# Batch 1's keys loaded earlier and tile 0's softmax on VectorE, in a chain of attention and two feed-forward layers

## The chip, the cores and the metric

The kernel runs on one core of one Trainium2 chip. The time is the device time of one execution in microseconds (us); lower is better. The core's engines work side by side, each through its own queue in order: TensorE (PE; its weight loads are shown as PEld), VectorE (DVE), ScalarE (ACT), GpSimd (POOL) and SyncE (SP), which issues nearly all transfers.

## The reference

```python
batch, n_heads, seq, head_dim, n_pack = 8, 8, 576, 64, 32
n_tokens, d_model, d_ff = 4608, 512, 2048

def sm_attn(qq, kk, vv):
    s = scale * np.matmul(qq, kk.transpose(0, 1, 3, 2))
    s = s - np.max(s, axis=-1, keepdims=True)
    a = np.exp(s)
    a = a / (np.sum(a, axis=-1, keepdims=True) + 1e-09)
    return np.matmul(a, vv)

p_packed = sm_attn(p, k, v)            # 32 learned queries a head
x = sm_attn(q, p_packed, p_packed)     # 576 queries a head
x = x.transpose(0, 2, 1, 3).reshape(4608, 512)
h = x @ moe_w_in                       # 512 -> 2048
x = (h * np.cos(h)) @ moe_w_out        # 2048 -> 512
h = x @ moe2_w_in
out = (h * np.tanh(softplus(h))) @ moe2_w_out
```

Inputs of attention are float32, the four weight matrices arrive as float64.

## The kernel before

**Tiles and steps.** The tokens of attention and of the first feed-forward layer go in 16 tiles of 288 tokens, two to a batch element. Each tile takes 16 steps, one for each 128 rows of d_ff, so a step is numbered n = 16 t + s. At step n PE computes layer 1 of (t, s) into one of four PSUM banks (`l1`, six matmuls L148 to L150 in `mm3`), ScalarE and VectorE work out h * cos(h) (`chain_first`, `chain_cos`: rounding L913, reduction L915 and L916, sine L922, product L928, which is the last reader of the bank), and three steps later PE does layer 2 (`l2`; for tile 0 in L953). The second feed-forward layer follows all tiles and is not touched.

**Weights by packed keys.** The value matrix of the second attention is folded into w_in: for each batch element, `w_unit` multiplies the packed values PK (L380) with w_in (L577) and splits the product into two halves (L593, L594); `l1` reads these. The float64 weights are turned into float32 by three operations: a Prelu on ScalarE (L520, L620), a shift on VectorE (L522, L621), a merge on VectorE (L526, L625). w_in comes in 16 pieces of 512 KB (L507) through four buffers, w_out in 16 pieces of 512 KB (L608) through the two buffers of `raw`. For tile 0 the merged w_out is used as it is (WM); L630 and L631 split it afterwards for the later tiles.

**Background work.** `k_unit(b, g)` packs the keys and values of four heads: four loads of keys into a `kr` buffer (L153), four loads of p into `pc` (L234), transposes on VectorE (L264, L159), scores on PE (L289), softmax, product with the values. `q_unit(t)` makes a tile's attention weights: scores (L431), transposes (L445), maximum and subtraction (L451, L452), exponential (L459), sum (L463), reciprocal (L466), product (L467), transpose (L471), and a split into a high half on ScalarE (L476) and a low half (L477). `at_ld`, `at_pe` and `at_ew` place each piece at a step; steps below 0 are the prologue. Batch 1's two groups have their stages from steps 13 and 18 on (`K1_OFF`).

**Order.** Within an engine the order is fixed when the program is built, by a planner that works from priorities (`tc.high_priority`) and its own estimate of the times. `tc.issue_after(x)` makes an instruction come later than x in it. `after_w` puts a load behind the last load of weights named so far, for steps up to 20. `behind(key)` does the same with an instruction kept in `marks`; ("act", 1, 0, 1) is the copy of the packed values of batch 0's second group.

Of the kernel before, what the change touches and what calls it, by code (L numbers as in the profile page):

```python
# [8 lines left out]
F32 = mybir.dt.float32  # L9
F32R = mybir.dt.float32r  # L10
I32 = mybir.dt.int32
AF = mybir.ActivationFunctionType
ALU = mybir.AluOpType
# [17 lines left out]
Q_LD = 2  # L31
W_LD = 2
K1_OFF = (13, 18)
K1_LD = 4
W01 = (28, 0.8)
WO_OFF = 0
WO_SPLIT = 13
# [14 lines left out]
Q_SUB0 = (0, 1, 2, 4, 5, 5, 6, 7)  # L52
K_LD0 = 2
Q_LD0 = 2
Q_DVE = (0, 0, 0)
X2_AT = 231
COMB = 240
HOLD_N = 32
# [24 lines left out]
SCALE = 1.0 / math.sqrt(D)  # L83
# [6 lines left out]
def build(tc, q, k, v, p, w1i, w1o, w2i, w2o, out):  # L90
    nc = tc.nc
    ctx = ExitStack()
    with ctx:
# [31 lines left out]
        quarter = wpool.tile([128, 1], F32, name="quarter")  # L125
        nc.vector.memset(quarter, 0.25)
        wpool.tile([128, 8], F32, name="gap_w")
        if WARM:
            warm = wpool.tile([128, 1], F32, name="warm")
# [79 lines left out]
        marks = {}  # L209

        def behind(key):
            ins = marks.get(key)
            return ExitStack() if ins is None else tc.issue_after(getattr(ins, "ins", ins))
# [181 lines left out]
        def q_unit(t, pre=None):  # L395
            st = {}
            b, half = t // 2, t % 2

            def loads():
                if pre:  # L400
                    st["raw"] = early_load(pre([128, 4, 512]), q[b], TT * half * D, False)
                    return
                r = kr_tile([128, 4, 544])
                st["raw"] = [r[:, 0:2], r[:, 2:4]]
                for e in range(2):
                    for g in range(2):
                        o = 64 * g + 32 * e
                        load_half(r[o : o + 32], q[b, 4 * g : 4 * g + 4], TT * half, e)

            def trans(i):  # L410
                if i == 0:
                    st["kt"] = kt_tile([128, 1152])
                trans2(st["kt"][:, 576 * i : 576 * i + 576], st["raw"][i])

            def s0():
                trans(0)

            def s1():
                trans(1)

            def e0_pe():
                st["kt"] = kt_tile([128, 1152])
                for h in range(4):
                    early_copy(st["kt"], early_trans(st["raw"], h, (0, 0, 1)), h, (0, 0, 1))

            def s2_pe():
                st["s"] = [ring() for _ in range(2)]

                def head(g, l):
                    h = PERM[b % 2][l]  # L430
                    return nc.tensor.matmul(  # L431
                        st["s"][g][32 * l : 32 * l + 32, :TT],
                        PK[(b, g)][64 * g : 64 * g + 64, 32 * l : 32 * l + 32],
                        st["kt"][64 * g : 64 * g + 64, TT * h : TT * h + TT],
                        start=True,
                        stop=True,
                    )

                todo = [lambda g=g, l=l: head(g, l) for g, l in sorted(((g, l) for g in range(2) for l in range(4)), key=lambda y: (-PERM[b % 2][y[1]], -y[0]))]
                rounds(st["s"][:1], st["kt"][:, 1152 - HOLD_N :], todo[0], todo[1:])  # L440

            def s2_ew():
                sq = tmp_tile([128, 2, TT])
                for g in range(2):
                    nc.vector.transpose(sq[:, g], st["s"][g][:, :TT])  # L445
                st["sq"] = sq
                st["sv"] = sq.rearrange("p g (a j) -> p (g a) j", j=32)

            def s3():
                mx = ap.tile([128, 18], F32, tag="mx", bufs=2, name=nm("mx"))  # L450
                nc.vector.tensor_reduce(mx, st["sv"], AX.X, ALU.max)  # L451
                (nc.vector if t < Q_DVE[0] else nc.gpsimd).tensor_tensor(st["sv"], st["sv"], mx.unsqueeze(2).to_broadcast([128, 18, 32]), ALU.subtract)  # L452

            def s4():
                with ExitStack() as es:
                    es.enter_context(tc.high_priority(offset=HP_EXP))
                    if CHAIN_EXP and lastexp[0] is not None:
                        es.enter_context(tc.issue_after(getattr(lastexp[0], "ins", lastexp[0])))
                    nc.scalar.activation(st["sq"], st["sq"], AF.Exp, scale=SCALE)  # L459

            def s5():
                sm = ap.tile([128, 18], F32, tag="sq", bufs=2, name=nm("sqs"))
                nc.vector.tensor_reduce(sm, st["sv"], AX.X, ALU.add)  # L463
                nc.vector.tensor_scalar(sm, sm, EPS, None, ALU.add)
                rs = ap.tile([128, 18], F32, tag="rq", bufs=2, name=nm("rq"))
                nc.vector.reciprocal(rs, sm)  # L466
                (nc.vector if t < Q_DVE[1] else nc.gpsimd).tensor_tensor(st["sv"], st["sv"], rs.unsqueeze(2).to_broadcast([128, 18, 32]), ALU.mult)  # L467

            def s6():
                at = tmp_tile([128, 2, TT])  # L470
                nc.vector.transpose(at.rearrange("p g s -> p (g s)"), st["sq"].rearrange("p g s -> p (g s)"))  # L471
                st["at"] = at

            def s7():
                hl = ap.tile([128, 2, 2, TT], F32R, tag="aT", bufs=2, name=nm("aT"))
                nc.scalar.copy(hl[:, 0], st["at"])  # L476
                (nc.vector if t < Q_DVE[2] else nc.gpsimd).tensor_tensor(hl[:, 1], st["at"], hl[:, 0], ALU.subtract)  # L477
                AT[t] = hl

            return loads, [  # L480
                (e0_pe, None) if pre else (None, s0),
                (None, None) if pre else (None, s1),
                (s2_pe, s2_ew),
                (None, s3),
                (None, s4),
                (None, s5),
                (None, s6),
                (None, s7),
            ]

# [109 lines left out]
        WM = []  # L600
        wm_last = [None]

        def wo1_unit(ft):
            st = {}

            def load():
                r = st["r"] = tp.tile([128, 512, 2], I32, tag="raw", bufs=2, name=nm("raw"))
                ins = nc.sync.dma_start(r.rearrange("p f t -> p (f t)"), w1o[128 * ft : 128 * ft + 128, :].bitcast(I32))  # L608
                last_w[0] = getattr(ins, "ins", ins)

            def words():
                if not WM:
                    for i in range(6):
                        x = wo_tile([128, 2, 512], F32)
                        WM.extend((x[:, 0], x[:, 1]))
                if ft == 12:
                    x = wab_tile(1, [128, 4, 512], F32)
                    WM.extend(x[:, i] for i in range(4))
                t = st["t"] = tp.tile([128, 512], I32, tag="tmp", bufs=TMP_BUFS, name=nm("cvt"))
                wm_last[0] = nc.scalar.activation(WM[ft], st["r"][:, :, 1].bitcast(F32), AF.Prelu, scale=2.0**-112, alpha=2.0**32)  # L620
                nc.vector.tensor_scalar(t, st["r"][:, :, 0], 29, None, ALU.logical_shift_right)  # L621

            def merge():
                mi = WM[ft].bitcast(I32)
                nc.vector.scalar_tensor_tensor(mi, mi, 3, st["t"], ALU.logical_shift_left, ALU.bitwise_or)  # L625

            def split():
                w = WO[(1, ft)] = wo_tile([128, 2, 512], F32R)
                with tc.issue_after(getattr(wm_last[0], "ins", wm_last[0])):
                    nc.scalar.copy(w[:, 0], WM[ft])  # L630
                nc.gpsimd.tensor_tensor(w[:, 1], WM[ft], w[:, 0], ALU.subtract)  # L631

            return load, [words, merge], split

        WST = {}
# [126 lines left out]
        def after_w(f, lim=CH_LIM):  # L762
            def run():
                if last_w[0] is None or STEP[0] > lim:
                    return f()
                with tc.issue_after(last_w[0]):
                    f()

            return run
# [7 lines left out]
        def at_ld(n, f):  # L777
            bg_ld.setdefault(n, []).append(f)
# [27 lines left out]
        for g in range(2):  # L806
            wo = lambda sh: wo_tile(sh, F32)
            wa = lambda sh: wab_tile(0, sh, F32)
            loads, vl, stages = k_unit(0, g, wo)
# [4 lines left out]
        loads, stages = q_unit(0, wa)  # L814
# [19 lines left out]
            at_ew(n + WO_SPLIT, split)  # L834
        for g, off in enumerate(K1_OFF):
            loads, vl, stages = k_unit(1, g, ld_tile)
            at_ld(off - K1_LD, after_w(loads))
            for i in range(3):
                at_ld(off + V_LD + i, after_w(vl[i]))
            place(stages, [off + i for i in K1_SUB])  # L840
# [9 lines left out]
        for j, n in enumerate(U_AT):  # L850
            loads, steps = w2o_unit(j)
# [12 lines left out]
        for pair in range(3):  # L864
# [3 lines left out]
            for b, g, off in zip((b0, b0, b0 + 1, b0 + 1), (0, 1, 0, 1), offs):  # L868
                loads, vl, stages = k_unit(b, g, ld_tile)
# [12 lines left out]
        for t in range(1, NT):  # L882
            n = Q_N[t - 1]
            loads, stages = q_unit(t)
# [438 lines left out]
```

## Time and profile before

| | |
|---|---|
| median of 3 runs | 1549.7 us (1548.65 to 1550.8) |
| profiled execution | 1550.71 us, its span in the trace 1548.9 us |
| mean granted TensorE clock | 0.987 |
| PE busy | 1479.0 us, 95% |
| VectorE, ScalarE, GpSimd busy | 71%, 57%, 40% |

An engine's busy time is the sum of its instructions; idle time is given with what ended it ("<-"). The granted clock is the share of full speed that TensorE was allowed.

### The profile page before, as it was taken

The page shows a single profiled execution, that of the slowest core. Times are in us where ns is not written, and L with a number is a line of the kernel's source. Part 1 is how long each engine was busy: PE and PEld are TensorE (multiplying, and loading weights), DVE is VectorE, ACT ScalarE, POOL GpSimd, SP SyncE. Part 2 cuts the span into 40 slices and gives each one's busy share as a digit, 9 for nine tenths or more (in the row PEclk, how much of TensorE's full clock was granted, in tenths as well). Part 3 has the DMA queues.
Part 4 walks back from the last instruction along what each step waited for, and adds up shares of the span by engine and source line. Part 5 has one row for each costly group of instructions (what it writes and reads, how often), then busy time and mean ns, then how long its engine had stood idle before and what let it go on. Part 6 is the DMA issues. An engine that isn't in the chain of part 4 may idle for free.

```text
span 1548.9 us, 28952 instructions
## 1 busy us (share of the span) xinstructions
PE 1479.0 (95%) x9922; PEld 1302.3 (84%) x9922; DVE 1103.8 (71%) x2080; ACT 888.7 (57%) x1834; POOL 623.8 (40%) x618
## 2 busy tenths in 40 slices
PE   7788999999999999999999999999999999999998
PEld 5568778899977999789999887888889898888997
DVE  4786667777677877687775778678668857766756
ACT  3576767667767767666765555334443534454443
POOL 0053333345543654536754666224421622352102
PEclk9899999999999999999999999999999999999999
DMA  7897576445648646623313757668868977876886
GB/s 270 263 259 187 170 184 164 129 111 171 176 132 217 176 139 171 194 89 91 105 51 113 250 212 251 190 201 242 263 214 231 310 216 218 243 213 217 232 263 201
DMA packets 247410, 299.20 MB, mean 193 GB/s; under 512 B 103648, under 2 KB 131040, under 8 KB 247264
## 3 DMA queue, kind: packets, MB, share of 16 engines
q1 hardware_dynamic: 244976, 296.21, 64.1%
q8 instruction: 79, 1.29, 0.4%
q10 hardware_dynamic: 2288, 1.15, 0.3%
q14 instruction: 67, 0.55, 0.1%
HBM read 240.65 MB, written 56.62 MB: 192 GB/s over the span
## 4 chain that ended last, share of the span: by engine, by line
PE 58%; DVE 8%; ACT 5%; DMA 3%; issue 3%; POOL 1%; SPq 1%; DVEq 0%; ACTq 0%; POOLq 0%
PE acc L149 10%; PE acc L150 10%; PE acc L148 10%; PE ps L148 9%; PE ps L149 9%; PE ps L150 9%; DVE r L916 2%; DVE r L915 1%; ACT r L922 1%; DVE r L928 1%; DMA raw<-in_moe_w_out_dram 1%; DVE wab L1020 1%; ACT L922 1%; DMA raw<-in_moe_w_in_dram 1%; PE ps L577 1%
## 5 line engine op out<-in xcount | busy, mean ns | idle before, releaser
L940 POOL TENSOR_TENSOR gh<-r,gh 128x288 fp32r<-128x288 f32 x240 | 199.6, 840 | 302.6 <-ACT gh L937 211.0
L1078 POOL TENSOR_TENSOR gh<-t,gh 128x512 fp32r<-128x512 f32 (+1 forms) x108 | 143.7, 1334 | 352.8 <-ACT gh L1077 343.1
L149 PE MATMUL acc<-gh,wo 128*128 128x288 f32 x960 | 282.5, 299 | 0.6 <-POOL gh L940 0.6
L150 PE MATMUL acc<-gh,wo 128*128 128x288 f32 x960 | 279.2, 297 | 0.0
L148 PE MATMUL acc<-gh,wo 128*128 128x288 f32 x960 | 261.9, 302 | 1.7 <-ACT gh L937 0.9
L149 PE MATMUL acc<-gh,T 128*128 128x512 f32 (+1 forms) x560 | 207.0, 371 | 2.1 <-DVE gh L1078 1.6
L148 PE MATMUL ps<-wab,ws 128*128 128x512 f32 (+1 forms) x560 | 206.0, 369 | 1.6 <-DMA ws<-wst 1.2
L149 PE MATMUL ps<-wab,ws 128*128 128x512 f32 (+1 forms) x560 | 206.4, 369 | 0.0
L150 PE MATMUL ps<-wab,ws 128*128 128x512 f32 (+1 forms) x560 | 205.3, 369 | 0.0
L150 PE MATMUL acc<-gh,T 128*128 128x512 f32 (+1 forms) x560 | 205.1, 369 | 0.0
L148 PE MATMUL ps<-aT,wab 128*128 128x288 f32 x512 | 163.7, 320 | 35.4 <-DVE r L928 21.3
L149 PEld LDWEIGHTS acc<-gh,wo 128*128 128x128 f32 x960 | 182.7, 190 | 6.9 <-issue 5.1
L1078 DVE TENSOR_TENSOR gh<-wo,gh 128x512 fp32r<-128x512 f32 (+1 forms) x160 | 128.0, 806 | 83.3 <-ACT gh L1077 82.8
L922 ACT ACTIVATE r<-r,halfpi 128x288 f32<-128x288 f32 x256 | 135.9, 535 | 88.2 <-DVE r L916 86.0
L148 PEld LDWEIGHTS acc<-gh,wo 128*128 128x128 f32 x960 | 172.5, 190 | 14.8 <-issue 6.1
L150 PEld LDWEIGHTS acc<-gh,wo 128*128 128x128 f32 x960 | 182.2, 190 | 2.1 <-issue 2.1
L148 PE MATMUL acc<-gh,T 128*128 128x512 f32 (+1 forms) x560 | 182.0, 369 | 1.0 <-DMA T<-tst 0.8
L928 DVE TENSOR_TENSOR r<-r,ps 128x288 f32<-128x288 f32 x240 | 107.3, 450 | 72.6 <-ACT r L922 72.3
L913 ACT ACTIVATE ki<-ps,quarter 128x288 int32<-128x288 f32 x256 | 124.6, 497 | 52.8 <-PE ps L150 41.2
L149 PE MATMUL ps<-aT,wab 128*128 128x288 f32 x512 | 154.0, 301 | 0.0
L150 PE MATMUL ps<-aT,wab 128*128 128x288 f32 x512 | 153.7, 300 | 0.0
L148 PEld LDWEIGHTS ps<-aT,wab 128*128 128x128 f32 x512 | 98.7, 193 | 62.2 <-DVE r L928 28.6
(193 smaller groups left out, 3061.7 us busy)
## 6 DMA issues: line engine op xcount, KB each, us to landing
T<-tst SPq DMA_DIRECT2D x280, 256.0 KB, 3.0
ws<-wst SPq DMA_DIRECT2D x224, 256.0 KB, 3.0
ld<-ws SPq DMA_DIRECT2D x80, 256.0 KB, 3.7
kr<-in_q_dram SPq DMA_DIRECT2D x60, 272.0 KB, 5.8
kr<-in_k_dram SPq DMA_DIRECT2D x56, 272.0 KB, 5.3
tst<-wt SPq DMA_DIRECT2D x56, 256.0 KB, 2.1
wst<-ws SPq DMA_DIRECT2D x56, 256.0 KB, 2.7
x2d<-xo SPq DMA_DIRECT2D x64, 144.0 KB, 1.7
```

Of the source, the lines that this page charges most:

```text
L148: nc.tensor.matmul(ps, l0, r0, start=first, stop=False, skip_group_check=more)
L149: nc.tensor.matmul(ps, l0, r1, start=False, stop=False, skip_group_check=more)
L150: nc.tensor.matmul(ps, l1, r0, start=False, stop=last, skip_group_check=more)
L577: return nc.tensor.matmul(st[b][32 * l : 32 * l + 32], PK[(b, g)][r : r + 64, 32 * l : 32 * l + 32], ms[h // 2]["m"][r : r + 64], start=Tr ...
L913: nc.scalar.activation(ki, st["h"], AF.Identity, bias=quarter, scale=1.0 / TWO_PI)
L915: nc.vector.scalar_tensor_tensor(r, ki, -TWO_PI, st["h"], ALU.mult, ALU.add)
L916: (nc.gpsimd if n % C_MOD in C_POOL else nc.vector).tensor_scalar(r, r, 1.570796, -4.712388, ALU.min, ALU.max)
L922: nc.scalar.activation(g, g, AF.Sin, bias=halfpi, scale=1.0)
L928: nc.vector.tensor_tensor(g, r, st["h"], ALU.mult)
L940: nc.gpsimd.tensor_tensor(gh[:, 1], st["g"], gh[:, 0], ALU.subtract)
L1020: (nc.gpsimd if k % 2 == 0 else nc.vector).tensor_tensor(x[:, a, 1, :n], src, x[:, a, 0, :n], ALU.subtract)
L1078: eng.tensor_tensor(hl[:, 1, :n], src, hl[:, 0, :n], ALU.subtract)
```

## The change

Five edits. `K1_LD` goes from 4 steps to 9 for both groups of batch 1's keys: their loads are placed at steps 4 and 9 instead of 9 and 14; their stages stay. `Q_DVE` goes from 0 to 1 for three operations of `q_unit`, so that tile 0's L452, L467 and L477 are VectorE's and not GpSimd's. Behind tile 0's exponential stands a sine of one column, which brings sine's table in. The Prelus of w_out's first two pieces come behind the packed values of batch 0's second group. All merges of w_out come behind tile 0's L477.

```diff
-K1_LD = 4
+K1_LD = (9, 9)
...
-Q_DVE = (0, 0, 0)
+Q_DVE = (1, 1, 1)
...
-                    nc.scalar.activation(st["sq"], st["sq"], AF.Exp, scale=SCALE)
+                    ins = nc.scalar.activation(st["sq"], st["sq"], AF.Exp, scale=SCALE)
+                    if t == 0:
+                        with tc.issue_after(getattr(ins, "ins", ins)):
+                            nc.scalar.activation(warm, quarter, AF.Sin)
...
-                (nc.vector if t < Q_DVE[2] else nc.gpsimd).tensor_tensor(hl[:, 1], st["at"], hl[:, 0], ALU.subtract)
+                ins = (nc.vector if t < Q_DVE[2] else nc.gpsimd).tensor_tensor(hl[:, 1], st["at"], hl[:, 0], ALU.subtract)
                 AT[t] = hl
+                marks[("aT", t)] = ins
...
-                wm_last[0] = nc.scalar.activation(WM[ft], st["r"][:, :, 1].bitcast(F32), AF.Prelu, scale=2.0**-112, alpha=2.0**32)
+                early = ("act", 1, 0, 1) if ft < 2 else None
+                with behind(early):
+                    wm_last[0] = nc.scalar.activation(WM[ft], st["r"][:, :, 1].bitcast(F32), AF.Prelu, scale=2.0**-112, alpha=2.0**32)
...
-                nc.vector.scalar_tensor_tensor(mi, mi, 3, st["t"], ALU.logical_shift_left, ALU.bitwise_or)
+                with behind(("aT", 0)):
+                    nc.vector.scalar_tensor_tensor(mi, mi, 3, st["t"], ALU.logical_shift_left, ALU.bitwise_or)
...
-            at_ld(off - K1_LD, after_w(loads))
+            at_ld(off - K1_LD[g], after_w(loads))
```

## Rows read from the trace of the kernel before

**Rows 1.** Page: TensorE's busy tenths in 40 equal slices of the span.

```profile
PE   7788999999999999999999999999999999999998
```

**Rows 2.** Busy times by stage: stretch, length, each engine, granted clock, DMA share, GB/s.

```profile
44.00:150.00 106.00, 91.65 (x628) 71.26 (x628) 79.95 (x178) 70.75 (x135) 34.21 (x29) 0.92 0.90 253
150.00:500.00 350.00, 332.88 (x3005) 292.08 (x3005) 247.41 (x577) 245.40 (x524) 143.12 (x165) 0.99 0.60 161
```

**Rows 3.** Timeline of tile 0's softmax: start, duration, instruction, idle before.

```profile
36.65 0.75 DVE L451 TENSOR_REDUCE mx<-tmp 128x18 f32<-128x576 f32 x1
37.49 1.16 POOL L452 TENSOR_TENSOR tmp<-tmp,mx 128x576 f32<-128x576 f32 x1 [36.18 <-DVE mx L451]
...
40.06 0.68 DVE L594 TENSOR_TENSOR wab<-ps,wab 128x512 fp32r<-128x512 f32 x1
...
41.28 1.16 POOL L467 TENSOR_TENSOR tmp<-tmp,rq 128x576 f32<-128x576 f32 x1 [2.63 <-DVE rq L466]
...
43.80 2.49 DVE L625 SCALAR_TENSOR_TENSOR wo<-wo,cvt 128x512 int32<-128x512 int32 x2
...
44.01 0.61 PE L148 MATMUL ps<-aT,wab 128*128 128x288 f32 x1 [6.60 <-ACT aT L476]
44.03 1.72 POOL L477 TENSOR_TENSOR aT<-tmp,aT 128x576 fp32r<-128x576 f32 x1 [1.59 <-ACT aT L476]
...
44.54 1.93 PE L577 MATMUL ps<-wab,pk 64*32 64x512 f32 x8
...
46.40 0.85 PE L148 MATMUL ps<-aT,wab 128*128 128x288 f32 x2
```

**Rows 4.** Timeline of ScalarE around the second early Prelu.

```profile
27.75 0.68 ACT L620 ACTIVATE wo<-raw 128x512 f32<-128x512 f32 x1
...
29.08 0.59 ACT L336 COPY tmp<-ps 128x512 f32<-128x512 f32 x1 [0.65 <-PE ps L328]
```

**Rows 5.** Timeline of ScalarE and TensorE around the first sine.

```profile
51.23 0.89 ACT L913 ACTIVATE ki<-ps,quarter 128x288 int32<-128x288 f32 x2
52.13 1.28 ACT L922 ACT_TABLE_LOAD   x1
53.43 0.54 ACT L922 ACTIVATE r<-r,halfpi 128x288 f32<-128x288 f32 x1
53.87 0.65 ACT L520 ACTIVATE wab<-wab 128x512 f32<-128x512 f32 x1
...
54.50 0.61 PE L148 MATMUL ps<-aT,wab 128*128 128x288 f32 x1 [4.06 <-DVE g L928]
```

**Rows 6.** Busy times of three short stretches, columns as in the second group.

```profile
56.00:64.00 8.00, 8.00 (x40) 5.82 (x39) 4.84 (x13) 3.56 (x8) 0.00 (x0) 0.88 1.05 246
92.00:96.00 4.00, 3.50 (x20) 2.78 (x19) 4.00 (x8) 3.47 (x7) 2.99 (x3) 1.00 0.34 105
120.00:124.00 4.00, 3.68 (x50) 3.33 (x51) 2.14 (x6) 2.02 (x5) 1.65 (x2) 0.50 0.88 241
```

**Rows 7.** Timeline of the sync queue's issues of w_out and batch 1's keys.

```profile
58.57 1.71 SPq L608 DMA_DIRECT2D raw<-in_moe_w_out_dram  x2
...
78.60 0.43 SPq L234 DMA_DIRECT2D pc<-in_p_dram  x1
...
86.79 9.42 SPq L608 DMA_DIRECT2D raw<-in_moe_w_out_dram  x4
96.26 0.42 SPq L234 DMA_DIRECT2D pc<-in_p_dram  x1
```

**Rows 8.** Timeline: three waits of TensorE and VectorE in tile 0.

```profile
82.63 0.63 PE L577 MATMUL ps<-wab,pk 64*32 64x512 f32 x4 [1.26 <-DVE wab L526]
...
114.59 0.31 DVE L264 STREAM_TRANSPOSE pp<-pc 128x128 f32<-128x128 f32 x1 [1.63 <-DMA pc<-in_p_dram]
...
117.78 0.40 PE L148 MATMUL ps<-aT,wab 128*128 128x288 f32 x1 [3.74 <-DVE r L928]
```

**Rows 9.** Issues of the first 130 us: count, size of one, time to landing.

```profile
kr<-in_k_dram SPq DMA_DIRECT2D x16, 272.0 KB, 5.8
```

## The prediction

> **What bounds the kernel now.** I read the page of the profile first. Over the whole span TensorE (PE) is busy almost throughout; apart from the last slice a 7 or an 8 stands only in the first four, some 150 us [rows 1]. Then busy times by stage: from 44 to 150 us PE works 91.65 us of 106, from 150 to 500 us 332.88 of 350 [rows 2]. All five edits touch what happens before about 120 us, so the question has two parts: how much of that early idle time goes, and whether it stays gone. After the head the kernel is a long queue of matmuls whose other work is tied to its own progress and not to a clock on the wall; a saving in the head should reach the end one for one, unless something in the head itself absorbs it.
>
> The timeline of the head shows three places where PE stands. First it waits for tile 0's softmax: PE had been idle 6.60 us when the first matmul of layer 1 started at 44.01, and the next matmul that needs the low half (L149, queued behind the L148 at 46.40) could not go before GpSimd ended L477 [rows 3]. Second, after four steps of layer 1 have filled the four banks of the ring, PE waits 4.06 us for the first bank, until 54.50; its last links are two roundings on ScalarE (L913), the load of sine's table (1.28 us) and the sine [rows 5]. Third, at 117.78 PE has waited 3.74 us for L928; inside that chain VectorE stood 1.63 us at 114.59 for a load of p (L264) [rows 8].
>
> The busy times of shorter stretches show the transfers: from 56 to 64 us the DMA engines are full (1.05), from 92 to 96 they are at 0.34 [rows 6]. The sync queue says why: four loads of w_out took it from 86.79 to 96.21, each waiting for one of two buffers, and batch 1's second group of keys, ordered behind the last of them, was issued only at 96.26 [rows 7].
>
> **The change, part by part.**
>
> *Three operations of tile 0 from GpSimd to VectorE.* None of these forms runs on VectorE before. The nearest row is L594, a two-input operation on 128x512 in 0.68 us [rows 3]; for 576 columns I estimate 0.68 x 576/512 = 0.77 us. L451 ends at 37.40 and L452 at 38.65, so the step takes 1.25 us; on VectorE 0.77, a saving of 0.48. L467 has the same length, so another 0.45 or so: 0.9 together. L477 lasts from 44.03 to 45.75, 1.72 us against 1.16 for the same shape in L452, beside the two L625 of 2.49 us; on VectorE it would be 0.77 behind the copy, a saving of 1.0. Sum 1.9 us. Above: PE had a block of L577 in between, 44.54 to 46.47, and only then went on; if the planner now puts layer 1 first, another 0.65 (46.40 less 45.75) comes on top, 2.55. Below: with L577 still in the gap only the first 0.9 counts. The 2.3 us of work added to VectorE lie where it waited for GpSimd; without that cover they would cost themselves and save nothing.
>
> *The first two conversions behind the packed keys, merges behind tile 0.* Two Prelus of 0.68 us, the second at 27.75, leave their place on ScalarE. After them ScalarE waited 0.65 us for PE's transposes anyway [rows 4], so nothing is gained there: 0. They now stand somewhere between the copy of the second packed keys and layer 1; put ahead of tile 0's exponential or its copy they would cost up to 2 x 0.68 = 1.36, so the first part's lower end is 0.9 - 1.36 = -0.5. I take 0, because ScalarE waits for VectorE and GpSimd through most of that chain. What waits behind the two Prelus are the merges, and behind them the second layer of tile 0, which follows layer 1 by three steps; that is past 54.50 and leaves some 10 us. The merges (L625) stood at 43.80, about where L477 will now be, and being on the same engine they only queue. 0.
>
> *Sine's table early.* The load leaves the chain of rows 5: ScalarE ended its L913 pair at 52.12, loaded from 52.13 to 53.41, and the sine started at 53.43. The bank comes free 1.28 us sooner. The number of loads does not fall: one moves to the idle time behind tile 0's exponential. That nothing in between brings the old table back is seen at 53.87, where a Prelu runs behind the sine with no load [rows 5]. I take the full 1.28; the lower end is 0, if another wait fills the place.
> The Trainium skill ("ScalarE: Activation LUTs", section "What ACT_TABLE_LOAD costs") puts a switch at the load of about 1283 ns plus a drain of about 1380 ns. The load of rows 5 agrees with the first number; of the drain nothing is seen, since the neighbours stand 0.01 and 0.02 us from it. By the Trainium skill the saving would be about 2.66 and the whole sum 1.4 better.
>
> *Batch 1's keys nine steps ahead instead of four.* Each group issues four loads of 272 KB [rows 9] and four small ones of p (L234, 16 KB each by the code): 1.18 MB. Both groups go through the sync queue, past loads and stores of weights; GpSimd's and ScalarE's queues are not touched.
> The second group moves from behind the last load of w_out (step 13's) to behind step 9's, so from 96.26 to about 86.8. It then runs in the stretch that had the engines at 0.34: 0.66 x 4 = 2.6 us of transfer time are regained, and what follows lands up to that much sooner. VectorE's 1.63 us at 114.59 is less than that, so I count it as gone: 1.6 (0 if the planner puts other work there; up to the whole 3.74).
> The first group moves from 78.60 to behind step 4's w_out load, about 60 [rows 7], in front of the last four w_in tiles and five w_out tiles. There the engines are full: 1.18 MB at 246 GB/s are 4.8 us by which all that follows can land later [rows 6]. PE is busy 8.00 of 8.00 there, so it does not wait at once; but at 82.63 it waited 1.26 us for the last quarter of w_in (L526) [rows 8], so lateness that lasts until then is paid in full. For cover: the same megabyte leaves the stretch from 78.60 on, just before that wait. Cost from 0 to 4.8; I take 0.5, near the lower end, because the total of bytes up to 96 us is unchanged.
>
> Sum: 1.9 + 1.28 + 1.6 - 0.5 = 4.3 us. The profiled execution took 1550.7 (its span of 1548.9 and 1.8 around it), so 1546.4; it lies 1.0 above the median of 1549.7, so 1545.4 us on that scale.
>
> **Rivals.**
>
> *The DMA takes the saving back.* The stretch from 56 us on is full of transfers, and a head that starts 3.2 us sooner only waits longer for weights. For it: the share of 1.05 in rows 6. Against it: PE at 8.00 of 8.00 in the same rows. Then about 1.2 us remain: 1548.5.
>
> *Keys in front of weights: slower.* Place: the last quarter of w_in at 82.63, and the last w_out loads. The first group costs its 4.8; the second its 4.8 less the 2.6 of the idle stretch, 2.2; and a wait that long makes PE fall to its lower clock, as from 120 to 124 us, where the granted clock was 0.50 (the 1.2 GHz level) after the wait of 3.74: 3.68 x 0.5 = 1.8. Together 8.8, against 1.9 + 1.28 from the head: 5.6 slower, 1555.3. It decides from a delay of about 6.3 us (3.2 and the 3.1 of the bound below). For it: the first group moves into a stretch that is full. Against it: nothing of it would show before PE's backlog is gone.
>
> *The clock comes too.* With shorter waits PE keeps 2.4 GHz in stretches where it had less: from 56 to 64 us 8.00 x (1 - 0.88) = 1.0, from 120 to 124 us 1.8 [rows 6]. 2.8 more: 1542.6. Against it: a wait of some 2 us or more stays at both places.
>
> *The drain.* If an engine-wide stop of 1.38 us comes with each load of a table, the first sine gains that too: 1544.0. Against it: the 0.01 and 0.02 us of rows 5. (The Trainium skill, "ScalarE: Activation LUTs", "What ACT_TABLE_LOAD costs", has this stop.)
>
> **How the numbers follow.** The sum as it stands 0.37, DMA takes it back 0.28, the clock comes too 0.20, keys in front of weights 0.12, the drain 0.03. A difference under 0.2% (3.1 us) is about what a measurement of this kernel can't tell from none: faster means under 1546.6, slower over 1552.8. The sum's own range is 1543 to 1548, of which I put 0.31 under 1546.6; with the clock, the drain and a small part of the second case, 0.56 faster. Slower is the fourth case and a little of re-ordered queues: 0.13. The rest, 0.31, is the same. For 8 in 10 the range goes from the clock with the upper ends of the first part and the third wait (1542.6 - 0.65 - 2.1 = 1539.8) to 1552, short of the slower case.
>
> **What would show it.** Right: VectorE rows L452, L467, L477 of 0.7 to 0.8 us; first matmul of layer 1 near 43 and its second within 1 us; a load of sine's table at about 39 and none before L922; PE's wait before step 4 under 3 us; keys of the second group issued before 90 us and the window behind 92 us full; no DMA wait at the L264 that stood at 114.59. Wrong: waits of L520 or L526 on w_in grown by microseconds between 65 and 85; a Prelu ahead of tile 0's exponential; an operation on VectorE much over 0.8 us; or a head that is 4 us sooner at 120 us and level by 500, which would mean that a saving does not travel.

## The result and the profile after

The changed kernel takes 1558.91 us, median of 5 runs (1555.77 to 1561.47), against 1549.7: a ratio of 1.0062, 95% interval 1.0045 to 1.0079. It is slower. The forecast was 1545.4 us with a range up to 1552.0, so both the sign and the range were wrong; the case that came about is the rival "keys in front of weights", given 0.12 and 1555.3 us. The profiled execution took 1555.77 us, its span 1554.0.

The page of the changed kernel, TensorE's busy tenths in 40 slices, and below it busy times by stage (stretch, length, each engine with its instructions, granted clock, DMA share, GB/s):

```profile
PE   6788999999999999998999999999999999999998
```

```profile
56.00:64.00 8.00, 7.77 (x44) 5.90 (x37) 5.01 (x12) 4.11 (x8) 0.00 (x0) 1.00 1.05 286
...
92.00:96.00 4.00, 4.00 (x27) 1.69 (x25) 1.62 (x4) 1.56 (x3) 0.59 (x1) 1.00 1.04 338
...
44.00:150.00 106.00, 86.79 (x541) 65.12 (x534) 74.09 (x163) 63.90 (x124) 29.68 (x26) 0.89 0.87 245
150.00:500.00 350.00, 334.20 (x3038) 293.56 (x3037) 246.10 (x574) 243.41 (x521) 143.60 (x165) 1.00 0.57 158
```

The loss is where the edits are: from 44 to 150 us PE works 4.86 us less than in [rows 2], and after that about as much. Two forecasts made from [rows 6] hold: from 56 to 64 us the clock is 1.00 (2.4 GHz) where it was 0.88, and the gap of the DMA engines behind 92 us is filled (1.04 for 0.34). Neither helped.

The timeline of the head, as in [rows 3] and [rows 5]:

```profile
35.18 0.75 DVE L451 TENSOR_REDUCE mx<-tmp 128x18 f32<-128x576 f32 x1
35.97 0.76 DVE L452 TENSOR_TENSOR tmp<-tmp,mx 128x576 f32<-128x576 f32 x1
...
36.76 0.68 ACT L459 ACTIVATE tmp<-tmp 128x576 f32<-128x576 f32 x1 [1.58 <-DVE tmp L452]
37.46 1.28 ACT L462 ACT_TABLE_LOAD   x1
...
38.86 0.57 ACT L597 CAST wab<-ps 128x512 fp32r<-128x512 f32 x1
39.47 0.69 DVE L598 TENSOR_TENSOR wab<-ps,wab 128x512 fp32r<-128x512 f32 x1 [1.24 <-ACT wab L597]
...
40.27 0.27 DVE L469 RECIPROCAL rq<-sqs 128x18 f32<-128x18 f32 x1
40.57 0.76 DVE L470 TENSOR_TENSOR tmp<-tmp,rq 128x576 f32<-128x576 f32 x1
...
42.90 0.61 PE L148 MATMUL ps<-aT,wab 128*128 128x288 f32 x1 [9.16 <-ACT aT L479]
...
50.46 0.54 ACT L929 ACTIVATE r<-r,halfpi 128x288 f32<-128x288 f32 x1
...
52.03 0.40 PE L148 MATMUL ps<-aT,wab 128*128 128x288 f32 x1 [2.44 <-DVE g L935]
```

The operations on VectorE take 0.76 us each, the sine at 50.46 has no load in front of it, and PE's second wait fell from 4.06 to 2.44 us. But the softmax itself became longer. From the start of the maximum (L451) to layer 1's first matmul it is 42.90 - 35.18 = 7.72 us; in [rows 3] it is 44.01 - 36.65 = 7.36. The weight cast L597 stands behind the new table load, VectorE waits 1.24 us for it at L598, and the reciprocal is queued behind L598.

The sync queue, as in [rows 7]. Its second w_out load of the pair at 58.57 (piece 7, counted from 0) was issued by 60.28 before; here it is the one at 69.12:

```profile
57.80 0.33 SPq L612 DMA_DIRECT2D raw<-in_moe_w_out_dram  x1
59.18 0.33 SPq L234 DMA_DIRECT2D pc<-in_p_dram  x1
...
68.69 0.31 SPq L153 DMA_DIRECT2D kr<-in_k_dram  x1
69.12 0.37 SPq L612 DMA_DIRECT2D raw<-in_moe_w_out_dram  x1
...
85.11 0.43 SPq L234 DMA_DIRECT2D pc<-in_p_dram  x1
...
103.99 1.57 SPq L153 DMA_DIRECT2D kr<-in_q_dram  x3
105.86 0.35 SPq L612 DMA_DIRECT2D raw<-in_moe_w_out_dram  x1
...
106.79 0.37 SPq L612 DMA_DIRECT2D raw<-in_moe_w_out_dram  x1
```

Eight loads of the first group took the queue from 59.18 to 69.12. The w_out load behind them was issued some 9 us later than before, but by the landing times in the two traces it landed 5.5 us later, at 75.47 against 69.98; the four pieces of w_out after it landed 4.8 to 5.4 us later than before, and the four pieces of w_in behind the group 5.4 to 5.6. The last two w_out loads, over by 96.21 before, left at 105.86 and 106.79, behind batch 2's keys and tile 2's queries (103.99), and landed 15.8 and 15.7 us later. What waited then, in the timelines of the three engines (PE, VectorE, ScalarE):

```profile
86.57 6.55 PE L960 MATMUL acc<-g,wo 128*128 128x288 f32 x16 [4.37 <-DVE g L935]
93.05 1.06 PE L581 MATMUL ps<-wab,pk 64*32 64x512 f32 x8
...
114.23 5.84 PE L960 MATMUL acc<-g,wab 128*128 128x288 f32 x16 [2.85 <-DVE wab L632]
...
125.30 0.40 PE L148 MATMUL ps<-aT,wab 128*128 128x288 f32 x1 [4.66 <-DVE r L935]
...
73.00 0.31 DVE L264 STREAM_TRANSPOSE pp<-pc 128x128 f32<-128x128 f32 x1 [1.73 <-DMA pc<-in_p_dram]
...
87.26 0.68 DVE L530 SCALAR_TENSOR_TENSOR wab<-wab 128x512 int32<-128x512 int32 x1
...
75.49 0.68 ACT L626 ACTIVATE wo<-raw 128x512 f32<-128x512 f32 x1 [3.65 <-DMA raw<-in_moe_w_out_dram]
...
112.78 0.67 ACT L626 ACTIVATE wab<-raw 128x512 f32<-128x512 f32 x1 [4.24 <-DMA raw<-in_moe_w_out_dram]
```

ScalarE stands 3.65 and 4.24 us for pieces of w_out; the matmul that needs the second of them, L960, waits for its merge. The transpose of p that waited at 114.59 in [rows 8] now waits at 73.00: early transposes were also put early on VectorE.

The same places before, on PE and VectorE (the L577 that follows at 82.63 is in [rows 8]):

```profile
77.32 4.04 PE L953 MATMUL acc<-g,wo 128*128 128x288 f32 x16
...
81.80 0.68 DVE L526 SCALAR_TENSOR_TENSOR wab<-wab 128x512 int32<-128x512 int32 x1
```

PE's queue has another order here. Before, L577 (w_in's product) and layer 1 of step 10 followed when 64 matmuls of layer 2 were done; in the change 80 stand in front of them, the last 16 being those at 86.57. The merge of w_in that L577 waited for at 82.63 ended 5.5 us later (87.94 against 82.48); its product started 10.4 us later, at 93.05. So the late weights account for 5.5 us there, about half, and the order for the rest. By step 12 the number of matmuls of layer 2 in front is the same again (80), and the delay is 4.6 us. Also, the 16 matmuls at 86.57 took 6.55 us where 16 took 4.04 before: behind the wait of 4.37 us the granted clock was 0.63 (86.50 to 93.20), and 1.00 at 77.30 to 81.40 before.

### The profile page after: what moved, and what is told of

It reads as the page before. It is cut to its first block, busy times and chain, and to the rows that moved or that the text cites. A ratio compares the mean times of both kernels' runs of the same rounds, so it can differ in the third digit from the quotient of the medians.

```text
span 1554.0 us, 28944 instructions
## 1 busy us (share of the span) xinstructions
PE 1477.5 (95%) x9922; PEld 1300.1 (84%) x9922; DVE 1107.0 (71%) x2083; ACT 887.4 (57%) x1835; POOL 618.6 (40%) x615
## 4 chain that ended last, share of the span: by engine, by line
PE 51%; DVE 5%; ACT 2%; issue 1%; POOL 1%; DMA 1%; SPq 0%; DVEq 0%; ACTq 0%; POOLq 0%
PE acc L149 9%; PE acc L150 9%; PE acc L148 9%; PE ps L148 8%; PE ps L149 8%; PE ps L150 8%; DVE wab L1027 1%; DVE r L923 1%; POOL gh L1085 1%; DVE r L922 1%; DVE t L1216 0%; ACT wab L1026 0%; DMA raw<-in_moe_w_in_dram 0%; ACT r L929 0%; ACT gh L1084 0%
## 5 line engine op out<-in xcount | busy, mean ns | idle before, releaser
L935 DVE TENSOR_TENSOR r<-r,ps 128x288 f32<-128x288 f32 x240 | 107.2, 449 | 77.0 <-ACT r L929 76.7
L920 ACT ACTIVATE ki<-ps,quarter 128x288 int32<-128x288 f32 x256 | 124.7, 496 | 43.8 <-PE ps L150 33.0
```

The source lines that it names most:

```text
L920: nc.scalar.activation(ki, st["h"], AF.Identity, bias=quarter, scale=1.0 / TWO_PI)
L935: nc.vector.tensor_tensor(g, r, st["h"], ALU.mult)
```

## The experiments

All runs of a group share their runs of the kernel before. One table serves them all. "Step n" is the start of step n's rounding (L913, L920) against before, in us; "piece 7" and "piece 15" are the starts of those w_out pieces' Prelus (L620, L626) against before, pieces counted from 0; all of it from the rows of each profiled execution. The ratio is over all timed runs. Tile 0's maximum starts between 35.18 and 39.02 in these executions (36.65 before), so a step's figure holds an uncertainty of a microsecond or so. Whole executions of the kernel before lie between 1543.42 and 1556.44 us in these runs; for the end, then, the ratio counts, and step 255 is one execution of each.

| run | step 3 | step 10 | step 18 | step 26 | step 255 | piece 7 | piece 15 | ratio, interval |
|---|---|---|---|---|---|---|---|---|
| the change | -2.4 | +9.1 | +8.6 | +10.0 | +6.8 | +4.7 | +15.2 | 1.0062 [1.0045, 1.0079] |
| e1_head | -2.3 | -1.6 | -0.5 | -1.6 | -0.5 | -1.8 | +0.3 | 1.0022 [1.0011, 1.0034] |
| e2_keys | -0.3 | +2.1 | +7.2 | +8.5 | +7.0 | +4.8 | +13.7 | 1.0091 [1.0074, 1.0108] |
| e3_first_group | -1.0 | +9.1 | +6.7 | +15.1 | +14.9 | +5.4 | +3.6 | 1.0110 [1.0095, 1.0125] |
| e4_second_group | -0.8 | -0.6 | +4.8 | +5.7 | +9.0 | -0.9 | +13.7 | 1.0065 [1.0052, 1.0077] |
| e5_chain | -3.1 | +9.4 | +5.5 | +6.2 | +4.5 | +2.6 | +8.0 | 1.0028 [1.0013, 1.0043] |
| g_hold | -0.5 | +6.3 | +5.4 | +6.2 | +2.8 | +3.7 | +11.1 | 1.0044 [1.0027, 1.0061] |
| h_p_early | -0.1 | +8.8 | +5.1 | +7.3 | +4.6 | +5.9 | +14.5 | 1.0041 [1.0026, 1.0056] |
| j_idle | -0.1 | +1.8 | +6.9 | +8.1 | +8.4 | -0.4 | -0.8 | 1.0067 [1.0044, 1.0091] |
| m_three_repairs | -0.7 | +7.6 | +5.5 | +5.1 | +7.0 | +5.2 | +9.5 | 1.0037 [1.0020, 1.0054] |
| h_p_before | +2.4 | +3.7 | +8.2 | +6.3 | +5.8 | +2.3 | +6.3 | 1.0042 [1.0024, 1.0060] |
| f_sin_only | -0.1 | +2.9 | +2.3 | +1.2 | +3.6 | +1.5 | +3.3 | 1.0012 [0.9994, 1.0029] |
| f_dve_only | -2.1 | -2.5 | -2.6 | -2.2 | +0.7 | -3.2 | -0.7 | 1.0017 [1.0001, 1.0034] |
| s_late | -1.1 | -0.5 | -0.2 | -0.4 | 0.0 | -0.2 | -0.2 | 0.9996 [0.9980, 1.0013] |
| s_late_dve | -2.9 | -3.5 | -3.3 | -2.4 | -0.5 | -3.5 | -1.2 | 1.0003 [0.9989, 1.0016] |
| s_late_head | -2.3 | -1.7 | -0.8 | -1.2 | -1.1 | -1.9 | +0.6 | 1.0007 [0.9992, 1.0023] |
| s_late_change | -4.2 | +6.0 | +6.0 | +7.4 | +7.1 | +1.5 | +12.6 | 1.0040 [1.0026, 1.0054] |

**The change taken apart.** Theory A: the early keys cost, by standing in front of weights. Rival B: the head's edits cost. A1 blames the first group's eight loads, A2 the second group, which lets batch 2's keys and tile 2's queries past the last w_out loads.

e1_head, the change with the keys at their old steps:

```diff
-K1_LD = (9, 9)
+K1_LD = (4, 4)
```

> The change without its key loads: batch 1's keys stay at 4 steps ahead, the four edits of the head stay. Theory A (the early keys stand in front of the weights in the sync queue and cost the time): the head's saving is seen alone, layer 1's fifth step about 2.5 us sooner than before and carried to the end, 1545 to 1548 us. Theory B (the head's edits cost the time, by work added to VectorE or by another order of the queues): about 1559 us, as the whole change.

e2_keys, the kernel before with the keys alone:

```diff
-K1_LD = 4
+K1_LD = 9
```

> The kernel before with the key loads alone at 9 steps ahead. Theory A: the loss without the head's saving, 1560 to 1563 us. Theory B: about 1550 us, as before.

e3_first_group, the change with the first group alone early:

```diff
-K1_LD = (9, 9)
+K1_LD = (9, 4)
```

> The change with only the first group of batch 1's keys early (9 and 4 steps). In the sync queue the last four loads of w_out stay together, and batch 2's keys stay behind them. Theory A1 (the first group's eight loads in front of w_in and w_out cost most): 1553 to 1558 us. Theory A2 (batch 2's keys and tile 2's queries, which the second group lets go ahead of the last two loads of w_out, cost most): 1545 to 1549 us.

e4_second_group, the change with the second group alone early:

```diff
-K1_LD = (9, 9)
+K1_LD = (4, 9)
```

> The change with only the second group early (4 and 9 steps). In the sync queue batch 2's keys and tile 2's queries go ahead of the last two loads of w_out, as in the whole change; the first group stays behind step 9's load. Theory A1: 1545 to 1549 us. Theory A2: 1553 to 1558 us.

With the head alone w_out's pieces 7 and 15 come within 1.8 us of their old times, with the keys alone 4.8 and 13.7 us late: A holds for most of the loss, and B has a small part (1.0022). But e1_head's 1551.96 us is above A's range (1545 to 1548): the head's own saving isn't there. Each group delays the pieces behind its own place: the first is seen at piece 7 and step 10, where the second leaves no trace; the second at piece 15 and from step 18 on. So A1 and A2 are both true, but the costs don't add: the first group alone ends later than both together, at 1565.08 us, 7 above A1's range.

Step 10 is not a clean measure of late weights, because PE's queue has the other order (80 matmuls of layer 2 ahead of it) in the change, in e3_first_group and in every repair but j_idle. In e2_keys 72 stand ahead, piece 7 is as late as in the change, and step 10 is only 2.1 us late. At step 12, where 80 are ahead in all of these, the delays are 4.6 us (the change), 6.0 (e3_first_group), 3.3 (e2_keys) and -1.9 (e4_second_group).

**Repairs of the change, one at a time.** Theory V puts the loss at step 10 on VectorE's wait at L264 (73.00); rival L on the late weights, by the places that the loads take in the sync queue. e5_chain tests A2: batch 2's loads stay behind w_out's.

e5_chain, the change with `after_w` holding loads of later steps too:

```diff
-CH_LIM = 20
+CH_LIM = 24
```

> The whole change, with batch 2's keys and tile 2's queries chained behind the last load of w_out as well (the chain's limit at step 24 instead of 20), so that they can't go ahead of it. Theory A2 (those loads delay the last two of w_out): step 18 of layer 1 is no later than before by more than 2 us, 1549 to 1553 us. Theory A1 (the first group alone): the time stays at 1557 to 1565 us.

g_hold, the change with the first group's transposes (L264 and both L159, the second stage likewise) behind step 12's reduction:

```diff
-                nc.vector.transpose(pp, st["pc"].rearrange("p h d -> p (h d)"))
-                st["pp"] = pp
-                trans(0)
+                with behind(("r", 12) if b == 1 and g == 0 else None):
+                    nc.vector.transpose(pp, st["pc"].rearrange("p h d -> p (h d)"))
+                    st["pp"] = pp
+                    trans(0)
...
```

> The whole change, with VectorE's transposes of the first group ordered behind step 12's reduction, so that VectorE does not stand at them while the keys are still under way (it stood 1.73 and 0.87 us at 73.00 and 74.51, in front of the chain of steps 8 and 9). Theory V (this wait in VectorE's queue makes the loss at step 10): step 10 comes 4 us or more sooner than in the change (95.2). Theory L (late weights make it): step 10 stays within 2 us of 95.2. For the end both expect 1552 to 1560 us.

h_p_early, the change with batch 1's loads of p taken out of `loads` and handed in at step -3:

```diff
+P1_AT = -3
...
+            if b == 1:
+                at_ld(P1_AT, p_loads)
```

> The whole change, with the eight loads of p (16 KB each) of batch 1's two groups taken out of the sync queue's full stretch and handed in at step -3. The keys' own eight loads of 272 KB stay nine steps ahead. Theory L (places, not bytes: every load waits for the landing of the eighth before it, and four of the eight places go to 16 KB): w_out's piece 7, issued at 69.1 in the change, is issued before 66, and 1550 to 1555 us. Bytes alone: less than 1 us of change, 1557 to 1560 us.

j_idle, the change with the whole first group at step -3 and the second back at 4 steps:

```diff
-K1_LD = (9, 9)
+K1_LD = (16, 4)
```

> The change with the first group's keys at step -3 (16 steps ahead), which puts them into the stretch from 28 to 44 us where the DMA engines were at 0.00 to 0.40, and the second group at 4 steps as before. Theory A: nothing of weights stands behind them, so the loss is gone and the stretch from 78 us on is lighter by 1.18 MB: 1545 to 1551 us. Rival: what costs is the early transposes on VectorE or a new order of the queues, wherever the loads stand: 1555 us or more.

In e5_chain the sync queue and VectorE show that the four w_out loads are together again, but behind the second group, and that a new wait for p comes:

```profile
91.47 13.26 SPq L612 DMA_DIRECT2D raw<-in_moe_w_out_dram  x4
...
117.45 0.31 DVE L264 STREAM_TRANSPOSE pp<-pc 128x128 f32<-128x128 f32 x1 [3.61 <-DMA pc<-in_p_dram]
```

Piece 15 gained 7.2 us on the change, step 18 3.1: A2 is part of the cost and not all. Step 18 is still 5.5 us late, where A2 allowed 2, and 1554.91 us lies between the ranges of both. g_hold brought step 10 from +9.1 to +6.3 (step 12 from +4.6 to +2.2), so V explains 2.8 us of it; what is left is late weights and PE's other order together, so neither V nor L is met as it stands. h_p_early took p's four small loads out of the first group, and the w_out load at 69.12 left at 66.55, 2.6 us sooner; but it landed at 76.63, where it landed at 75.47 in the change, and piece 7 was still 5.9 us late. 66.55 and the 1556.83 us lie between what places and bytes alone were expected to give.

j_idle decides against theory A of its own text (1545 to 1551 us) and for the rival there, another order of the queues wherever the loads stand (1555 or more): it took 1558.98 us (1.0067, where e1_head, the same but for the first group's place, has 1.0022). The first group went into the idle stretch ahead of layer 1, and w_out's pieces kept their times (-0.4, -0.8); still step 12 was 10.5 us late and the end +8.4. Its timeline shows another reason, eight weight splits in front of step 12's rounding on ScalarE and a wait for p in front of its reduction on VectorE:

```profile
99.91 4.24 ACT L637 CAST wo<-wo 128x512 fp32r<-128x512 f32 x8
...
103.92 0.31 DVE L264 STREAM_TRANSPOSE pp<-pc 128x128 f32<-128x128 f32 x1 [1.50 <-DMA pc<-in_p_dram]
104.06 0.88 ACT L920 ACTIVATE ki<-ps,quarter 128x288 int32<-128x288 f32 x2
...
111.63 0.64 PE L166 MATMUL ps<-kt,ident 128*128 128x32 f32 x2 [8.04 <-DVE g L935]
```

PE then stood 8.04 us for a product (L935) at 111.63. So on-time weights alone don't make the early keys free: the planner writes another order around them. How much of the change's own loss is such an order, and how much the late weights, was not separated; what e1_head and e2_keys show is that the early keys cause it.

**The repairs together, and small loads by themselves.** Theories S (three separate places) and Q (the early keys cost wherever the wait shows) are told in the text on record; its 4.3 us for e5_chain should read 3.8.

m_three_repairs is the change with the diffs of e5_chain, g_hold and h_p_early:

> The change with all three repairs together: the first group's transposes held behind step 12's rounding, batch 2's loads and tile 2's queries kept behind the last w_out loads, and batch 1's small p loads handed in before the layer starts. Alone they took 3.8, 4.3 and 2.7 us off step 26's delay of 10.0 us. Theory S (three separate places): step 26 within 1 us of before, ratio 0.999 to 1.001. Rival Q (the early keys themselves, 2.2 MB in front of the weights, cost about 6 us wherever the wait shows): step 26 still at least 4 us late, ratio 1.003 to 1.005.

h_p_before is the kernel before with h_p_early's diff alone:

> The kernel before with one edit of another kind: batch 1's sixteen-kilobyte p loads handed in before the layer starts, keys four steps ahead as before, so that eight places of SP's rotation come free ahead of the weights and no large transfer moves forward. Theory Q (places and bytes in front of the weights are what the keys cost): the last w_out loads issued about 2 us sooner than at 86.79 to 96.21, step 18 one to three us earlier, ratio 0.998 to 0.999. Rival N (the weights' times are not set there): step 18 within 0.5 us of before, ratio 0.9995 to 1.001.

Together they leave step 26 5.1 us late and the ratio at 1.0037: Q, within the bounds it gave. Three repairs of 3.8, 3.8 and 2.7 took off 4.9, hardly more than one. h_p_before missed both theories: the eight small loads, moved ahead of layer 1, made the kernel slower. They took the sync queue from 15.28 to 25.44 us, in front of w_out's first two loads (15.22 before, 25.48 here). In this kernel the Prelus of those two pieces still stand ahead of the packed values on ScalarE, which waited 2.24 us for the first; the copy behind them came at 31.48 (L336, 29.08 in [rows 4]), and tile 0's maximum began at 39.02 (36.65 before, 37.46 at most in the runs of the first group of experiments). So the run starts with a loss of its own at the head and doesn't test Q. The four w_out loads also took the queue longer than in [rows 7]. ScalarE and the sync queue:

```profile
29.05 0.66 ACT L639 ACTIVATE wo<-raw 128x512 f32<-128x512 f32 x1 [2.24 <-DMA raw<-in_moe_w_out_dram]
...
87.43 14.19 SPq L627 DMA_DIRECT2D raw<-in_moe_w_out_dram  x4
```

**The head's edits, one at a time.** T, R and P are told in the texts on record.

f_sin_only, the kernel before with this part of the change:

```diff
-                    nc.scalar.activation(st["sq"], st["sq"], AF.Exp, scale=SCALE)
+                    ins = nc.scalar.activation(st["sq"], st["sq"], AF.Exp, scale=SCALE)
+                    if t == 0:
+                        with tc.issue_after(getattr(ins, "ins", ins)):
+                            nc.scalar.activation(warm, quarter, AF.Sin)
```

> The kernel before with one edit alone: the sine's table loaded behind tile 0's exponent. Its engines otherwise run the same order as before. Theory T (a saving at the head reaches the end when nothing is reordered): step 0's rounding comes about 1.3 us earlier, step 30's about 1.3 us earlier, and the time is about 1.3 us less, ratio near 0.999. Rival R (the head's saving is lost again at the weights of steps 4 to 20, whose loads have their own times): step 30 within 0.4 us of before, ratio 1.000.

f_dve_only, the kernel before with this part:

```diff
-Q_DVE = (0, 0, 0)
+Q_DVE = (1, 1, 1)
```

> The kernel before with one edit alone: the first tile's three GpSimd operations on VectorE. Theory T: layer 1's first matmul about 1.1 us earlier, and if the saving travels, step 30 about 1 us earlier, ratio 0.999. Rival P (this edit also makes the planner write another order further on, which loses the gain around steps 24 to 29 as in the run of the head's edits alone): step 12 at least 1 us earlier, step 29 not earlier than before, ratio 1.001 to 1.003.

From tile 0's maximum to layer 1's first matmul f_dve_only takes 6.39 us (42.66 - 36.27), 0.97 less than before; f_sin_only takes 8.68 (45.57 - 36.89), 1.32 more. The load saved in front of the first sine is given back in the softmax, so step 3 comes out at -0.1 and T falls for it; R isn't tested, since there was no gain to lose, and step 30 is 1.2 us late. For f_dve_only P holds: step 24 is 3.9 us early, step 29 0.6 late. What stands there on ScalarE, first in the kernel before and then in f_dve_only:

```profile
145.90 0.50 ACT L913 ACTIVATE ki<-ps,quarter 128x288 int32<-128x288 f32 x1 [1.27 <-PE ps L150]
...
146.42 1.28 ACT L312 ACT_TABLE_LOAD   x1
```

```profile
142.83 1.28 ACT L312 ACT_TABLE_LOAD   x1 [2.11 <-DVE sm L306]
...
145.09 0.50 ACT L913 ACTIVATE ki<-ps,quarter 128x288 int32<-128x288 f32 x1
```

The exponents of batch 2's softmax went ahead of step 25's rounding instead of behind it. That the order differs is shown; that it is what costs the 4.5 us between steps 24 and 29 wasn't tried.

**The sine's table one place later.** Theory C: the early load cost because a cast stood behind it; D: a load stops the chain wherever it stands; K: the keys set the end of the whole change.

```diff
-                nc.scalar.copy(hl[:, 0], st["at"])
+                cp = nc.scalar.copy(hl[:, 0], st["at"])
+                if t == 0:
+                    with tc.issue_after(getattr(cp, "ins", cp)):
+                        nc.scalar.activation(warm, quarter, AF.Sin)
```

s_late is the kernel before with this:

> The kernel before, with the sine's table loaded behind the copy that ends tile 0's softmax on ScalarE. Theory C (the early load cost 1.3 us because a weight cast stood behind it): from tile 0's maximum to layer 1's first matmul 7.36 us as before, against 8.68 with the load behind the exponent, and step 3 about 1.3 us earlier. Rival D (a table load stops the chain wherever it stands): again 8.0 us or more. The time, if the saving travels: ratio 0.999; if not, 1.000.

s_late_dve has f_dve_only's diff too:

> As the run before it, and tile 0's three GpSimd operations on VectorE. Theory C: tile 0's maximum to layer 1's first matmul 6.4 us, to layer 2's first matmul 15.0 us (17.85 before, 16.3 with the VectorE operations alone). If the head's gain travels: step 30 two to three us earlier, ratio 0.998. If softmax's place around steps 24 to 29 takes it, as with the VectorE operations alone: step 24 at least 3 us earlier, step 30 within 1 us of before, ratio 1.000 to 1.002.

s_late_head is e1_head with this in place of its own early sine:

> The change without its early keys, the sine's table loaded behind tile 0's copy. Theory C: tile 0's maximum to layer 2's first matmul about 15 us (16.67 with the load behind the exponent). Time: between the head's edits alone (ratio 1.0022) and 0.998, by whether the gain passes steps 24 to 29.

s_late_change is the change with this in place of its own:

> The change as it is, keys nine steps ahead, with the sine's table loaded behind tile 0's copy. Theory K (the early keys set the end, and the head only waits longer for the weights): the head 1.3 us shorter, w_out's last piece still over 10 us late, step 26 still 8 us late or more, ratio 1.005 to 1.007. Rival: the repaired head comes through, ratio 1.004 or less.

The timeline of s_late:

```profile
36.85 0.75 DVE L451 TENSOR_REDUCE mx<-tmp 128x18 f32<-128x576 f32 x1
...
39.47 0.57 ACT L596 CAST wab<-ps 128x512 fp32r<-128x512 f32 x1
...
44.17 1.28 ACT L479 ACT_TABLE_LOAD   x1
44.21 0.61 PE L148 MATMUL ps<-aT,wab 128*128 128x288 f32 x1 [6.96 <-ACT aT L476]
```

The cast follows the exponential again and the softmax takes 7.36 us, to the hundredth what it took before; with the VectorE operations 6.39 (43.08 - 36.69). C holds. To layer 1's first matmul of step 3, the one at 54.50 in [rows 5] (the texts on record call it layer 2's first), the three take 15.47 (s_late_dve), 15.79 (s_late_head) and 15.69 us (s_late_change), where before took 17.85 and the change 16.85. That whole gain doesn't reach the end: s_late has -0.9 at step 4 and -0.2 at step 5, whose rounding stands on ScalarE behind the Prelu of a w_in piece that landed at 65.76 us, against 65.97 before; s_late_dve passes that place (-4.9 at step 5) and has -4.0 at step 24 and -0.5 at step 29. All three kernels without early keys are level with before. s_late_change falls between its theories: piece 15 is 12.6 us late as K expects, but step 26 is 7.4 us late, not 8, and the ratio of 1.0040 is the rival's own bound, with an interval that reaches into K's range.

No version of these beats the kernel before.

## Why the prediction was wrong, by its own steps

**First key group: the step that failed.** The group's bytes over the throughput of a full stretch gave a bound of 4.8 us; the forecast took 0.5 of it, "because the total of bytes up to 96 us is unchanged". The bound was right in size and the choice in it wrong. The pieces of w_out and w_in right behind the group landed 4.8 to 5.6 us later, though the head was a microsecond or two early, and the lighter stretch from 78.60 on did not give that back. ScalarE, in order, stood for a piece of w_out (3.65 us at 75.49); the merge that PE had waited 1.26 us for at 82.63 [rows 8] ended 5.5 us later; and step 12 came 4.6 us late. Step 10 came 9.1 us late (e3_first_group the same, e4_second_group -0.6), but that holds another order in PE's queue, with a wait of 4.37 us at 86.57, which the forecast did not have. VectorE's early transposes were 2.8 us of the 9.1 (g_hold). The forecast priced the loads alone; j_idle shows that the order around them can cost as much with the weights on time.

**Second key group: wrong sign.** The gap of [rows 6] was filled, and the wait at 114.59 went from there; but the expected -1.6 became a loss. The group let further loads ahead of the last two w_out loads, which the forecast saw only as 2.2 us in the rival. Piece 15 came 15.2 us late, and alone the group made step 26 5.7 us late (ratio 1.0065).

**Sine's table: -1.28 was right where it was taken from and wrong where it was put.** "The idle time behind tile 0's exponential" wasn't idle for the chain: L594 at 40.06 [rows 3] stands between the sum and the reciprocal on VectorE and needs a cast that ScalarE does in that place. Cost 1.32, net 0. (The wait in [rows 5] stands behind three steps of layer 1 and one block of L577, which hold the four banks, and not behind four steps; the 1.28 us are the same.)

**Operations on VectorE: mis-sized.** Forecast -1.9, with -0.9 as the lower end if PE's block stayed in the gap. It stayed, and 0.97 was measured up to layer 1's first two matmuls and 1.5 up to the one at 54.50 (16.32 against 17.85); 0.76 us for each operation against 0.77 estimated.

**Prelus and merges: 0 is not contradicted.** s_late_head and s_late_dve, which differ by them, are 1.0007 and 1.0003, with overlapping intervals.

**"A saving travels one for one" failed for gains.** Losses mostly kept their size through later tiles (step 26 to 96 of the change: +10.0 to +10.3, step 255 +6.8). Gains of about 3 to 4 us at step 24 ended within about 1 us of zero; in f_dve_only and s_late_dve most went between steps 24 and 29, where the order differs.

**The rivals.** "Keys in front of weights" had the places right, and two of its terms show: about 5 us behind the first group, and a lower clock behind a wait (6.55 us for 16 matmuls against 4.04). That its 1555.3 us lies within 4 us of the result is partly luck: the keys alone cost about 14 us (e2_keys), not 8.8, the head's gain of 3.2 that it took off was a loss of 0.2% (e1_head), and the two don't add. It was given too little, because the argument against it, that PE was busy throughout, only says when the wait begins. "The drain" is not seen: in s_late the copy, the load and the next activation follow each other at 43.48, 44.17 and 45.46 and the softmax is no longer; with the load out of the chain step 3's first matmul came 1.11 us sooner after the maximum (16.74 against 17.85), where load and drain together would have given 2.66. The Trainium skill ("ScalarE: Activation LUTs", "What ACT_TABLE_LOAD costs") lists such a stop, and no run here shows it.

What stays open: how the change's loss divides between late weights and the other order of the queues, why the first group alone costs more than both, and how much of steps 24 to 29 is order.

## What to carry to other kernels

Before moving a load forward, write down what it is put in front of in the queue and when each of those is needed. Take its bytes over the throughput as the delay of what stands right behind it (4.8 us estimated, 4.8 to 5.6 measured here); that the total of bytes is the same later on did not take it back. Where a planner writes the order, a moved load can also bring another order of the engines' queues, so look there before blaming the transfers. Work moved into an engine's idle time is free only if no instruction queued behind it feeds the chain: read the next instruction of that engine and who waits for it. A gain at the head of a kernel is not yet one at its end: follow it step by step and see where it goes.

## What the runs showed of the hardware

A load of 16 KB held up the sync queue's next issues about as much as one of 272 KB where transfers were dense. The DMA view of the changed kernel from 58 to 70 us gives issues, size of one and median time to landing:

```profile
kr<-in_k_dram SPq DMA_DIRECT2D x4, 272.0 KB, 7.9
...
pc<-in_p_dram SPq DMA_DIRECT2D x4, 16.0 KB, 7.8
```

In that stretch each issue of the group began within 0.1 us of the landing of the eighth transfer before it in the queue (59.18 behind 59.16, 68.69 behind 68.68). The waits of the sync queue:

```profile
SPq L234 <- DMA wab<-in_moe_w_in_dram: 2.6, 2, 1.8
SPq L153 <- DMA kr<-in_q_dram: 2.1, 2, 1.3
SPq L153 <- DMA raw<-in_moe_w_out_dram: 2.1, 1, 2.1
```

(line, what it waited for, us in total, times, longest). So a small load costs a place in the order of the issues: without the four loads of p, 64 KB in all, the next w_out load left 2.6 us sooner (h_p_early). At the landing no gain shows: 76.63 us against 75.47, with the DMA engines full (1.05 and 1.04 from 58 to 70 us). The comparison is rough, because tile 0's maximum was 2.2 us later in that execution (37.33 against 35.18).
